# Start-up fills, weight loads, masked copies and the last products of a fused recurrence, gated MLP and attention kernel

## The chip, the cores and the metric

The kernel runs on one core of a Trainium2 chip. The metric is the device time of one launch in microseconds (us). The engines are called as in the profile: PE is TensorE, DVE is VectorE, ACT is ScalarE, POOL is GpSimd, and SP is SyncE, which issues nearly all transfers.

## The reference

Three stages follow each other. B = 4 batches, H = 8 heads, S = 768 positions, D = 48 channels a head.

```
state = 0                                    # per batch and head, 48 x 48
for t in range(S):                           # 1: a gated linear recurrence
    cur = outer(u * k[t], v[t])
    y[t] = r[t] @ (state + cur)
    state = w[t][:, None] * state + outer(k[t], v[t])
x = y of all heads, as (B, S, 384)
h = relu(x @ w_in)                           # 2: 384 -> 1024
c = 3-tap convolution of h along S, one filter a channel
x = (h * sigmoid(c)) @ w_out                 # 1024 -> 384
logits = x @ w_gate                          # 3: attention with 4 experts, the best 2 of 4 a row
out = sum over e of w[e] * (softmax(causal(q[e] k[e]^T / 8)) @ v[e]) @ wo[e]
```

## The kernel before

**Stage 1 and 2 (`phase1`).** The recurrence is computed in chunks of 128 positions. A unit is one batch, one half of the sequence (3 chunks) and one pair of heads: 32 units, `u` = 0 to 31, each in a slot of code (`slot`, line 559). All engines follow the written order there (`manual_schedule`): an engine takes its instructions strictly one after another. For a unit, `load` (line 129) brings one tile `wkr` of 1156 columns: 388 of decays w, 384 of k, 384 of r. DVE scans the decays forward (`scan_d`, tile Dp, with the constants cD) and backward (`scan_f`, tile Fp, with cF), and multiplies them into Q and K. In each slot PE transposes K (`trans`, line 327, into a tile `m`), multiplies k*r by u (`m<-u_c,wkr`, the bonus of the own position, only for u < 12), forms the 6 score blocks (`scores`, into two one-bank tiles `sc`), the state (`state`) and the output of the unit before (`yout`). ACT puts the bonus on the diagonal of a tile AT (`blocks`, 6 instructions for u < 6). DVE then lays the scores above it where a mask allows (`masked`, line 322): two copies with a predicate, 128x384 each, one a head. At the end of each slot ACT and DVE cut the output of the unit before into a high and a low part (`rows`), and SP moves it into X.

The weights arrive raw (`load_w`, 768 KB pieces, tile `rawt`) and are converted in the slots around: `conv0_w` and `conv1_w` on DVE, ACT and POOL, `conv2_w` on ACT, `conv3_w` on DVE. From slot 5 on the MLP's products run between these (`mlp1`, line 436; `mlp2`, line 513). `slot` prepares unit u+1 while it finishes unit u.

**Before the first slot** POOL fills cD, cF, a tile of ones for the mask and the four state tiles Ss (lines 172 to 186). SP issues the loads of units 0, 1 and 2 (each `wkr` in two pieces), the small `u_c` (0.8 KB in runs of 4 bytes), `u_b`, and, from slot 0, the first raw weights.

**Stage 3 (`Attention.run`).** Sixteen units `j`, each two heads and one half of the rows. The order is a scheduler's, not written out. `soft` forms scores in a tile `st` (two banks, two buffers), DVE adds the mask and takes the minimum, ACT exponentiates into A. For the unit before, `transp` multiplies A by the row's factor `rs`, transposes it on PE (tile `t`) and copies it out as T; `av` multiplies by V; `proj_out` (line 1142) multiplies the high and low parts of the result O by two parts of `wo`, six products a row block, and stores a block of the output. The multiplication of A by `rs` is on DVE up to unit 12 and on POOL from unit 13 (`SCALED_ON_POOL`, line 46).

```
1112            if self.unit >= SCALED_ON_POOL:
1113                nc.gpsimd.tensor_tensor(at, at, rs[:, q:q + 1].to_broadcast(...), op=OP.mult)
1115                nc.vector.tensor_scalar(at, at, rs[:, q:q + 1], None, op0=OP.mult)
```

Of the kernel before, what the change touches and what calls it, by code (L numbers as in the profile page):

```python
# [23 lines left out]
C = 128  # L24
# [19 lines left out]
EARLY = 8  # L44
CARRY_ON_PE = 8
SCALED_ON_POOL = 13
# [60 lines left out]
def phase1(tc, nc, a, x2, ident, stat, lim, top, right, left2, at):  # L107
# [5 lines left out]
    ps_s = s1.enter_context(tc.tile_pool(name="ps_s", bufs=2, space=PSUM, side="left"))  # L113
# [15 lines left out]
    def load(u):  # L129
        b, h, hp = split(u)  # L130
        q = b * HP + hp
        x = ld.tile([128, NWKR], F32, name="wkr")
        if u not in (0, 1, 2, 28, 29, 30, 31):
# [33 lines left out]


    cD = cst.tile([128, CH, C + 1], F32, name="cD")
    cF = cst.tile([128, CH, C + 1], F32, name="cF")  # L170
    with tc.manual_schedule(engines={mybir.EngineType.Pool}):
        nc.gpsimd.memset(cD, 0.0)
        nc.gpsimd.memset(cD[:, :, 0:1], 1.0)
        nc.gpsimd.memset(cD[:, :, C:C + 1], TINY)  # L174
        nc.gpsimd.memset(cF, 0.0)
    ones3 = wk.tile([128, CH, C], F32, name="Q")
    nc.gpsimd.memset(ones3, 1.0)
    nc.gpsimd.affine_select(ones3, ones3, pattern=[[0, CH], [1, C]], compare_op=OP.is_gt, fill=0.0, base=0,
                            channel_multiplier=-1)
    msk = cst.tile([128, CH, C], U32, name="msk")  # L180
    nc.vector.tensor_copy(msk, ones3)
    Ss = []
    for i in range(HP):
        t = cst.tile([128, NC - 1, 64], F32, name=f"Ss{i}")
        nc.gpsimd.memset(t, 0.0)
        Ss.append(t)
# [3 lines left out]
    for u in (1, 2):  # L190
        load(u)
        load_v(u)
    u_b = cst.tile([128, HP, 2, D], F32, name="u_b")
    nc.sync.dma_start(u_b, bass.AP(tensor=a["u"].tensor, offset=a["u"].offset, ap=[[0, 128], [1, H * D]]))

# [29 lines left out]
    RW = {}  # L225

# [86 lines left out]
    def scores(u):  # L313
        t = T[u]
        sc = [ps_s.tile([128, CH, C], F32, name="sc") for j in range(2)]
        for c in range(CH):
            for j in range(2):
                p = slice(64 * j, 64 * j + 64)
                nc.tensor.matmul(sc[j][:, c], t["K"][p, c], t["Q"][p, c], start=True, stop=True)  # L319
        t["sc"] = sc  # L320

    def masked(u):
        t = T[u]
        for j, sc in enumerate(t["sc"]):
            nc.vector.copy_predicated(t["AT"][:, j], msk, sc)

    def trans(u):
        b, h, hp = split(u)
        t = T[u]
        n = CH - h  # L330
        m = ps_m.tile([128, CH * 128 + 2 * CH], F32, name="m")
        kt = m[:, 0:CH * 128].rearrange("p (c t) -> p c t", c=CH)
        for c in range(n):
            nc.tensor.transpose(kt[:, c], t["K"][:, c], ident)
        KT = t["KT"] = wk.tile([128, CH, 128], F32, name="KT")
        if u < BONUS_ON_PE:
            es = m[:, CH * 128:].rearrange("p (j c) -> p j c", j=2)
            for c in range(CH):
                nc.tensor.matmul(es[:, :, c], t["r"][:, c], u_c[:, hp], start=True, stop=True)
# [219 lines left out]
    def slot(u):  # L559
# [3 lines left out]
        for z, n, m in WS + WC2:  # L563
            if u == z - 1:
                load_w(n, m)
# [90 lines left out]
        if EARLY <= u < 2 * NU:  # L656
            check(u, 1)
# [12 lines left out]
    with tc.manual_schedule(engines=mine):  # L670
        scan_d(0)
# [236 lines left out]
class Attention:  # L908
    def __init__(self, tc, nc, a, x2, out, ident):
# [33 lines left out]

    P3 = ((0, 0), (0, 1), (1, 0))
# [163 lines left out]
    def transp(self, A, rs, T, qi):  # L1108
# [32 lines left out]

    def proj_out(self, b, O, t):
        nc = self.nc
        pt = self.ps_m.tile([128, 512], F32, name="m")
        m = 0
        for p in range(2):
            for oi, wi in self.P3:
                nc.tensor.matmul(pt[:, 0:DM], O[oi][:, p, t * C:(t + 1) * C], self.wo[wi][:, p], start=(m == 0),  # L1148
                                 stop=(m == 5))
                m += 1  # L1150
        ot = self.ap.tile([128, DM], F32, name="ot", bufs=3)
        if t in OUT_ON_DVE:
            nc.vector.tensor_copy(ot, pt[:, 0:DM])
        else:
            nc.scalar.activation(ot, pt[:, 0:DM], AF.Copy)
        nc.sync.dma_start(self.out[b, t * C:(t + 1) * C], ot)

    def run(self):
# [41 lines left out]
        def tail(j):  # L1200
# [4 lines left out]
            for e in range(2):  # L1205
                for q in range(3):
                    def f(e=e, q=q):
# [4 lines left out]
                        self.unit = j  # L1212
# [157 lines left out]
```

## Time and profile before

| | |
|---|---|
| median of 3 runs | 599.38 us (599.34 to 600.6) |
| profiled execution, its own time | 599.62 us |
| span of its instructions | 597.9 us |
| PE busy, its instructions | 567.4 us (95%), 4386 |
| PE weight loads busy | 508.6 us (85%) |
| DVE busy | 495.7 us (83%) |
| ACT busy | 397.1 us (66%) |
| POOL busy | 172.8 us (29%) |
| q1, the data queue | 89.53 MB, 51.7% of 16 engines |

The times of the profile are those of one execution, counted from the start of its span; its own time is 1.72 us more than its span. An engine's share over the whole span mixes stages with different limits, so shares are read by stretch. A row of the timeline gives start, duration, engine, line of the code, operation, tiles written and read, and a count.

### The profile page before, as it was taken

How to read it: one execution, taken by the hardware profiler on the slowest of the kernel's cores; microseconds unless marked ns; L12 is line 12 of the kernel's file. 1: busy time of each engine (PE TensorE's matmuls, PEld its weight loads, DVE VectorE, ACT ScalarE, POOL GpSimd, SP SyncE). 2: the span in 40 equal slices, each digit the busy share in tenths (PEclk: the TensorE clock that was granted, in tenths of full speed). 3: DMA queues.
4: the chain of work that ended last, by engine and by line, in shares of the span. 5: the costliest groups of instructions: out<-in, count | busy, mean ns of one | idle time of the engine just before them, and what ended most of it. 6: DMA issues, size and time to landing. Idle time of an engine off the chain costs nothing.

```text
span 597.9 us, 12391 instructions
## 1 busy us (share of the span) xinstructions
PE 567.4 (95%) x4386; PEld 508.6 (85%) x4386; DVE 495.7 (83%) x1153; ACT 397.1 (66%) x1015; POOL 172.8 (29%) x246
## 2 busy tenths in 40 slices
PE   4898989999999999999999999999999999999986
PEld 4686888999999999989999999697889787988644
DVE  6999999999999999999966865988767865875751
ACT  4986656767777788887776764766656565655622
POOL 3565552335435342424400000400120021004250
PEclk9759889999999999999999999999999999999999
DMA  7676425664747868676453436760476053605202
GB/s 237 229 253 208 161 77 143 191 172 125 223 123 225 295 198 285 205 225 185 128 139 101 118 87 166 201 143 1 121 198 158 28 130 96 145 28 147 67 1 86
DMA packets 47158, 90.41 MB, mean 151 GB/s; under 512 B 14320, under 2 KB 28656, under 8 KB 47088
## 3 DMA queue, kind: packets, MB, share of 16 engines
q1 hardware_dynamic: 47088, 89.53, 51.7%
q8 instruction: 37, 0.61, 0.4%
q14 instruction: 33, 0.27, 0.2%
HBM read 50.23 MB, written 9.44 MB: 100 GB/s over the span
## 4 chain that ended last, share of the span: by engine, by line
PE 65%; DVE 15%; ACT 7%; DMA 6%; issue 3%; POOL 2%; SPq 2%; ACTq 0%; DVEq 0%; POOLq 0%
PE hs L447 11%; PE x L521 11%; PE m L1012 8%; PE st L1086 6%; PE t L1120 5%; PE m L1136 5%; PE m L1042 4%; PE m L1148 3%; PE sc L319 2%; DMA sl<-kl 2%; DVE Dp L258 2%; PE m L397 2%; PE m L405 2%; DVE Fp L266 1%; PE m L352 1%
## 5 line engine op out<-in xcount | busy, mean ns | idle before, releaser
L447 PE MATMUL hs<-X,win 128*128 128x384 f32 (+1 forms) x576 | 118.4, 350 | 1.0 <-ACT ht L451 1.0
L447 PEld LDWEIGHTS hs<-X,win 128*128 128x128 f32 x576 | 99.2, 189 | 3.8 <-ACT ht L451 1.7
L521 PE MATMUL x<-gh,wout 128*128 128x386 f32 (+1 forms) x384 | 100.1, 342 | 0.0
L1100 ACT ACTIVATE A<-sm,mn 128x128 f32<-128x128 f32 (+5 forms) x96 | 63.7, 664 | 27.6 <-DVE mn L1099 27.6
L484 ACT ACTIVATE st<-ct 128x382 f32<-128x382 f32 (+1 forms) x64 | 33.7, 526 | 69.5 <-DVE ct L479 35.8
L1099 DVE CUSTOM_DVE_ANT_0 sm<-st,mask 128x128 f32<-128x128 f32 (+5 forms) x96 | 58.1, 619 | 22.6 <-PE st L1086 19.3
L302 POOL TENSOR_SCALAR_AFFINE_SELECT AT<-e 128x384 f32<-128x384 f32 x52 | 43.6, 859 | 108.9 <-DVE e L292 107.8
L521 PEld LDWEIGHTS x<-gh,wout 128*128 128x128 f32 x384 | 71.7, 193 | 0.0
L521 PE MATMUL x<-gl,wout 128*128 128x382 f32 (+1 forms) x192 | 65.6, 342 | 0.0
L1120 PE MATMUL t<-ident,A 128*128 128x128 f32 x336 | 53.2, 275 | 2.8 <-ACT T L1124 1.6
L1120 PEld LDWEIGHTS t<-ident,A 128*128 128x128 f32 x336 | 39.8, 140 | 10.0 <-issue 4.1
L1126 DVE COPY T<-t 128x128 f32<-128x128 f32 (+3 forms) x64 | 32.2, 503 | 18.4 <-PE t L1120 18.0
L1136 PE MATMUL m<-T,V 128*64 128x384 f32 (+2 forms) x288 | 45.9, 422 | 0.4 <-ACT T L1124 0.2
L1086 PE MATMUL st<-sk,sq 128*128 128x384 f32 (+3 forms) x128 | 43.8, 353 | 0.8 <-DVE mn L1099 0.5
L1086 PE MATMUL st<-sl,sq 128*128 128x384 f32 (+3 forms) x128 | 40.7, 328 | 2.8 <-DMA sl<-kl 2.7
L493 DVE SCALAR_TENSOR_TENSOR st<-st,ht 128x382 f32<-128x382 f32 (+1 forms) x64 | 36.4, 569 | 7.1 <-ACT st L484 5.4
L1124 ACT ACTIVATE T<-t 128x512 f32<-128x512 f32 (+3 forms) x64 | 28.5, 445 | 20.7 <-PE t L1120 20.4
L258 DVE TENSOR_TENSOR_SCAN Dp<-wkr,cD 128x387 f32<-128x387 f32 x32 | 39.1, 1221 | 3.6 <-POOL cD L174 3.6
L455 ACT ACTIVATE ct<-ht,cwk 128x382 f32<-128x382 f32 (+1 forms) x64 | 39.5, 618 | 2.1
L310 ACT ACTIVATE Fp<-wkr,lim 128x384 f32<-128x384 f32 x64 | 38.8, 607 | 0.3
L1136 PEld LDWEIGHTS m<-T,V 128*64 128x64 f32 x288 | 21.6, 136 | 20.2 <-issue 14.1
L508 DVE TENSOR_TENSOR gl<-st,gh 128x382 fp32r<-128x382 f32 (+1 forms) x64 | 35.6, 557 | 1.8 <-ACT gh L500 1.6
(148 smaller groups left out, 1316.4 us busy)
## 6 DMA issues: line engine op xcount, KB each, us to landing
wkr<-in_wkr SPq DMA_DIRECT2D x25, 578.0 KB, 4.2
v<-in_rkv SPq DMA_DIRECT2D x32, 192.0 KB, 4.1
rawt<-in_win SPq DMA_DIRECT2D x8, 768.0 KB, 6.1
rawt<-in_wout SPq DMA_DIRECT2D x8, 768.0 KB, 5.8
sk<-kh SPq DMA_DIRECT2D x32, 192.0 KB, 3.4
sl<-kl SPq DMA_DIRECT2D x32, 192.0 KB, 4.0
rn<-in_rkv SPq DMA_DIRECT2D x20, 288.0 KB, 3.7
x<-x SPq DMA_DIRECT2D x12, 384.0 KB, 4.3
```

Of the source, the lines that this page charges most:

```text
L258: nc.vector.tensor_tensor_scan(fl(t["Dp"]), t["w"][:, 0:NW], fl(cD), 0.0, op0=OP.mult, op1=OP.add)
L302: nc.gpsimd.affine_select(AT[:, j], t["e"][:, j][:, :, None].to_broadcast([128, CH, C]), pattern=[[0, CH], [1, C]], compare_op=OP.is_equal ...
L310: nc.scalar.activation(Fp[:, :, 0:C], wc, AF.Relu, bias=lim[:, z:z + 1], scale=(-1.0, 1.0)[z], accum_out=stat[:, 2 * u + z:2 * u + z + 1])
L447: nc.tensor.matmul(hs[:, 0:N], win[wi][:, f // 2, i, (f % 2) * 128:(f % 2 + 1) * 128], x[:, i, xi], start=(n == 0), stop=(n == 8))
L455: nc.scalar.activation(ct, ht[:, o:o + N], AF.Copy, scale=w[:, 1, f:f + 1])
L521: nc.tensor.matmul(acc[0][i][:, 0:N], wout[wi][:, f, i * 128:(i + 1) * 128], G[g][gi], start=(f == 0 and z == 0), stop=(f == NF - 1 and z ...
L1012: nc.tensor.matmul(pt[:, 0:HT], w[wi][:, i, p * 128:(p + 1) * 128], xs[xi][:, i, s], start=(m == 0), stop=(m == 8))
L1086: nc.tensor.matmul(st[:, z, 0:n], q[:, qi * C:(qi + 1) * C], k[:, z * n:(z + 1) * n], start=(i == 0), stop=(i == 1))
L1099: nc.vector.tensor_tensor_reduce(o3, i3, m3, 1.0, 3e38, op0=OP.add, op1=OP.min, accum_out=mn)
L1100: nc.scalar.activation(at, o3, AF.Exp, bias=mn, scale=-1.0, accum_out=rs[:, qi % 3:qi % 3 + 1])
L1120: nc.tensor.transpose(pt[:, ki - k0], at[:, ki * C:(ki + 1) * C], self.ident)
L1136: nc.tensor.matmul(po[o, lo:HT], V[:, ki, (2 * p + j) * 64:(2 * p + j + 1) * 64], Ts[j][:, ki, lo:], start=(ki == 0), stop=(ki == n - 1))
```

## The change

1. **Constants and mask.** DVE instead of POOL fills the ones, cD and cF. POOL keeps the triangular select that makes the mask of the ones, and the four Ss. The cast of the mask (`msk`) moves ahead of the first scan on DVE.
2. **Loads.** `wkr` of units 1 and 2 goes in one transfer each, and that of unit 1 stands ahead of v and u_c. The first raw weights stand right behind `wkr` of unit 2, before slot 0, and their first conversion moves within slot 1, to behind `keys`. `u_b` is loaded in slot 2. `wkr` of units 24 to 27 goes in two pieces instead of one.
3. **Unit 0 on PE.** The products with u_c come ahead of the transposes.
4. **Masked copy.** Both heads' scores lie in one tile of two banks, and one copy of 128x768 takes the place of two of 128x384 in all 32 units.
5. **Scaling of A.** POOL keeps only the first head of units 14 and 15, (14, 0) and (15, 0); unit 13 and the second heads of 14 and 15 go to DVE.
6. **Last products.** Of the last row group, nine of the eighteen products (those of the first pair of heads) are formed when the tail of the last unit begins, in the two `st` tiles. The other nine follow the last `av`, high parts first. The three blocks are evacuated by ACT, DVE and ACT; the third is stored from ACT's queue.

```
-EARLY = 8
-SCALED_ON_POOL = 13
+SCALED_ON_POOL = ((14, 0), (15, 0))
...
+    with tc.manual_schedule(engines={mybir.EngineType.Pool, mybir.EngineType.DVE}):
+        nc.vector.memset(ones3, 1.0)
+        nc.vector.memset(cD, 0.0)
+        nc.vector.memset(cD[:, :, 0:1], 1.0)
+        nc.vector.memset(cD[:, :, C:C + 1], TINY)
+        nc.vector.memset(cF, 0.0)
     load(0)
+    load(1)
     load_v(0)
...
+    load(2)
+    load_w("win", 0)
+    load_v(1)
+    load_v(2)
...
-        sc = [ps_s.tile([128, CH, C], F32, name="sc") for j in range(2)]
+        sb = ps_s.tile([128, 2, 512], F32, name="sc")[:, :, 0:CH * C]
+        sc = [sb[:, j].rearrange("p (c t) -> p c t", c=CH) for j in range(2)]
...
-        for j, sc in enumerate(t["sc"]):
-            nc.vector.copy_predicated(t["AT"][:, j], msk, sc)
+        nc.vector.copy_predicated(t["AT"].rearrange("p j c t -> p j (c t)"),
+                                  fl(msk)[:, None, :].to_broadcast([128, 2, CH * C]), t["sc"])
...
-            if u == z:
+            if u == z and u > 1:
                 conv0_w(n, m)
...
+        if u == 1:
+            conv0_w("win", 0)
...
-        if self.unit >= SCALED_ON_POOL:
+        if self.unit in SCALED_ON_POOL:
...
+    def proj_sum(self, pt, O, t, p, parts=P3):
+        for oi, wi in parts:
+            self.nc.tensor.matmul(pt, O[oi][:, p, t * C:(t + 1) * C], self.wo[wi][:, p],
+                                  start=(p == 0 and (oi, wi) == (0, 0)), stop=(p == 1 and oi == 1))
...
+            if j == NJ - 1:
+                pts = []
+                def early():
+                    z = [self.ps_s.tile([128, 2, 512], F32, name="st") for _ in range(2)]
+                    for t in range(3):
+                        pts.append(z[t % 2][:, t // 2, 0:DM])
+                        self.proj_sum(pts[t], OS[b], 3 * h + t, 0)
+                def final():
+                    for parts in self.P3[0:2], self.P3[2:3]:
+                        for t in range(3):
+                            self.proj_sum(pts[t], OS[b], 3 * h + t, 1, parts)
+                    ots = [self.ot(pts[t], t == 1) for t in (0, 1, 2)]
+                    for t in range(3):
+                        queue = self.nc.scalar if t == 2 else self.nc.sync
+                        queue.dma_start(self.out[b, (3 * h + t) * C:(3 * h + t + 1) * C], ots[t])
+                todo.insert(0, early)
+                todo.append(final)
```

The start of DVE's order before, up to the first products of unit 1 (Q on the mask's row is the tile of ones, which shares its name with the queries):

```order
L258 SCALAR_TENSOR_TENSOR Dp<-wkr,cD 128x387
L261 RECIPROCAL cF<-Dp 128x3
L278 TENSOR_TENSOR Q<-wkr,Dp 128x384
L181 CAST msk<-Q 128x384
L266 SCALAR_TENSOR_TENSOR Fp<-wkr,cF 128x387
```

And the same start of DVE's order now:

```order
L162 MEMSET Q 128x384
L163 MEMSET cD 128x387
L164 MEMSET cD 128x3
L165 MEMSET cD 128x3
L166 MEMSET cF 128x387
L676 CAST msk<-Q 128x384
L249 SCALAR_TENSOR_TENSOR Dp<-wkr,cD 128x387
L252 RECIPROCAL cF<-Dp 128x3
```

Five fills and the cast of the mask now stand ahead of the first scan.

SP's first transfers now (before, lines 137 to 205 in this order: `wkr` of unit 0 in two, v, u_c, `wkr` of units 1 and 2 in two pieces with a v behind each, u_b, raw weights):

```order
L136 DMA wkr<-in_wkr 128x388
L136 DMA wkr<-in_wkr 128x768
L133 DMA wkr<-in_wkr 128x1156
L144 DMA v<-in_rkv 128x384
L173 DMA u_c<-in_u 48x4x1 x2
L133 DMA wkr<-in_wkr 128x1156
L192 DMA rawt<-in_win 128x768
L144 DMA v<-in_rkv 128x384 x2
```

The whole `wkr` of unit 1 has moved to before u_c, and the raw weights to before the v of unit 1.

PE's order now, from the last scores of the last unit (`st<-sl`) to the next transposes (A_7480 and A_7550 are the two heads of unit 14); before, eleven transposes stood here in a row:

```order
L1094 MATMUL st<-sl_7304,sq_7218 128x384
L1152 MATMUL st<-wo_4383,O_7469 128x384
L1152 MATMUL st<-wo_4384,O_7469 128x384
L1152 MATMUL st<-wo_4383,O_7470 128x384
...
L1128 MATMUL t<-ident,A_7480 128x128 x5
L1152 MATMUL st<-wo_4383,O_7469 128x384
L1152 MATMUL st<-wo_4384,O_7469 128x384
L1152 MATMUL st<-wo_4383,O_7470 128x384
L1128 MATMUL t<-ident,A_7480 128x128 x2
L1128 MATMUL t<-ident,A_7550 128x128 x4
```

Nine products with `wo` (three more stand at the "...") now lie among the transposes of unit 14.

DVE's order there now, with the copies T<-t of the transposes and the multiplications of A (`TENSOR_SCALAR A`), which were on POOL:

```order
L1114 TENSOR_TENSOR rs<-rs,ex 128x3
L1123 TENSOR_SCALAR A_7550<-A_7550,rs 128x512
L1123 TENSOR_SCALAR A_7550<-A_7550,rs 128x640
L1123 TENSOR_SCALAR A_7550<-A_7550,rs 128x768
L1112 TENSOR_SCALAR rs<-rs 128x3
L1113 RECIPROCAL rs<-rs 128x3
L1114 TENSOR_TENSOR rs<-rs,ex 128x3
L1107 ISA sm,mn<-st,mask 128x256
L1107 ISA mn 128x1
L1134 COPY T_7625<-t 128x4x128
L1148 TENSOR_TENSOR O_7470<-m,O_7469 128x384
L1107 ISA sm,mn<-st,mask 128x384
```

The last two maskings (`sm<-st`), which free the two `st` tiles, stand behind three multiplications that were not on this engine.

## Rows read from the trace of the kernel before

**Rows 1.** Busy time by stretch: stretch, PE, PEld, DVE, ACT, POOL, PEclk, DMA, GB/s
```profile
20.00:110.00 90.00, 80.61 (x663) 71.95 (x661) 88.73 (x151) 63.02 (x169) 47.51 (x64) 0.83 0.54 171
110.00:222.00 112.00, 111.94 (x1051) 106.15 (x1050) 110.67 (x207) 81.95 (x208) 49.13 (x60) 1.00 0.66 197
```

**Rows 2.** Chain of waits, 60 to 222 us: start, duration, engine, tile, line
```profile
118.33 1.48 DVE Dp L258
...
133.06 1.78 PE hs L447 x9
```

**Rows 3.** Chain of waits, 7 to 20 us
```profile
6.90 0.48 DVE K L273
...
7.51 0.87 PE m L334 x3
...
12.69 1.09 PE m L339 x6
...
14.24 1.85 ACT AT L300 x6
...
20.00 1.51 DVE Dp L258
```

**Rows 4.** Timeline of the first 8 us; in brackets the idle time before and its end
```profile
0.81 0.87 SPq L137 DMA_DIRECT2D wkr<-in_wkr  x2
...
1.50 0.42 POOL L172 MEMSET cD<- 128x387 f32 x1
...
2.20 0.92 SPq L164 DMA_DIRECT2D u_c<-in_u  x2
...
3.62 0.96 DVE L258 TENSOR_TENSOR_SCAN Dp<-wkr,cD 128x387 f32<-128x387 f32 x1 [3.62 <-POOL cD L174]
3.88 1.01 POOL L178 TENSOR_SCALAR_AFFINE_SELECT Q<-Q 128x384 f32<-128x384 f32 x1
...
5.23 0.35 DVE L181 CAST msk<-Q 128x384 uint32<-128x384 f32 x1
```

**Rows 5.** DMA issues, 0 to 3.15 us: size of each, us from issue to landing
```profile
wkr<-in_wkr SPq DMA_DIRECT2D x1, 384.0 KB, 3.2
wkr<-in_wkr SPq DMA_DIRECT2D x1, 194.0 KB, 2.4
...
u_c<-in_u SPq DMA_DIRECT2D x2, 0.8 KB, 2.9
```

**Rows 6.** Timeline of DVE, 72 to 74 us
```profile
72.01 0.95 DVE L95 SCALAR_TENSOR_TENSOR wm<-rawt,wm 128x768 int32<-128x768 int32 x1
72.88 1.07 DVE L325 COPY_PREDICATED AT<-msk,sc 128x384 f32<-128x384 uint32 x2
73.83 0.55 DVE L418 TENSOR_TENSOR Y<-m,Y 128x384 fp32r<-128x384 f32 x1
```

**Rows 7.** Busy time by stretch, line 325 (masked copies) alone
```profile
20.00:110.00 90.00, 9.49 (x18) 0.83 0.54 171
```

**Rows 8.** Busy time by stretch, 570 to 580 us
```profile
570.00:580.00 10.00, 7.58 (x48) 4.86 (x48) 5.95 (x13) 3.42 (x8) 5.71 (x8) 1.00 0.00 1
```

**Rows 9.** Waits, 568 to 580 us: who for whom, us in total, times, longest
```profile
PEld t L1120 <- POOL A L1113: 2.4, 3, 1.0
```

**Rows 10.** Timeline, 561.7 to 571 us
```profile
567.05 1.37 DVE L1106 TENSOR_TENSOR rs<-rs,ex 128x3 f32<-128x3 f32 x1
...
568.57 3.68 POOL L1113 TENSOR_TENSOR A<-A,rs 128x512 f32<-128x512 f32 x3 [0.16 <-DVE rs L1106]
```

**Rows 11.** Groups of DVE by form, 330 to 598 us: count, busy us, mean ns
```profile
L1115 DVE TENSOR_SCALAR A<-A,rs 128x768 f32<-128x768 f32 x12 | 7.4, 615 | 0.0
```

**Rows 12.** Timeline of the end
```profile
588.55 3.78 PE L1148 MATMUL m<-wo,O 128*128 128x384 f32 x18
...
592.37 0.49 ACT L1155 ACTIVATE ot<-m 128x384 f32<-128x384 f32 x1 [0.50 <-PE m L1148]
```

**Rows 13.** DMA issues after 592.4 us
```profile
out_dram<-ot SPq DMA_DIRECT2D x1, 192.0 KB, 3.0
```

More of the change, by code (lines that the diff above doesn't have):

```diff
@@ L112, in phase1 @@
     wk = s1.enter_context(tc.tile_pool(name="wk", bufs=3, side="left"))
-    ps_s = s1.enter_context(tc.tile_pool(name="ps_s", bufs=2, space=PSUM, side="left"))
+    ps_s = s1.enter_context(tc.tile_pool(name="ps_s", bufs=1, space=PSUM, side="left"))
     ps_m = s1.enter_context(tc.tile_pool(name="ps_m", bufs=2, space=PSUM, side="left"))
@@ L132, in load @@
         x = ld.tile([128, NWKR], F32, name="wkr")
-        if u not in (0, 1, 2, 28, 29, 30, 31):
+        if 0 < u < 24:
             nc.sync.dma_start(x, a["wkr"][q, h])
@@ L156, in load_rk @@
                                   for o in (0, 2 * CH * D))
+    cD = cst.tile([128, CH, C + 1], F32, name="cD")
+    cF = cst.tile([128, CH, C + 1], F32, name="cF")
+    msk = cst.tile([128, CH, C], U32, name="msk")
+    ones3 = wk.tile([128, CH, C], F32, name="Q")
+    with tc.manual_schedule(engines={mybir.EngineType.Pool, mybir.EngineType.DVE}):
[4 more added lines that the diff above has]
+        nc.vector.memset(cF, 0.0)
     load(0)
+    load(1)
     load_v(0)
@@ L166, in phase1 @@
     wide = a["win"].dtype == U64
[L169 to L181, printed above, removed]
     Ss = []
     for i in range(HP):
-        t = cst.tile([128, NC - 1, 64], F32, name=f"Ss{i}")
-        nc.gpsimd.memset(t, 0.0)
-        Ss.append(t)
+        Ss.append(cst.tile([128, NC - 1, 64], F32, name=f"Ss{i}"))
     Bd = []
@@ L189, in phase1 @@
         Bd.append(cst.tile([128, NC - 1, 128], F32, name=f"Bd{i}"))
-    for u in (1, 2):
-        load(u)
-        load_v(u)
     u_b = cst.tile([128, HP, 2, D], F32, name="u_b")
-    nc.sync.dma_start(u_b, bass.AP(tensor=a["u"].tensor, offset=a["u"].offset, ap=[[0, 128], [1, H * D]]))
     WC = 2 * DM
@@ L332, in trans, with sums @@
         kt = m[:, 0:CH * 128].rearrange("p (c t) -> p c t", c=CH)
+        es = m[:, CH * 128:].rearrange("p (j c) -> p j c", j=2)
+        def sums():
+            for c in range(CH if u < BONUS_ON_PE else 0):
+                nc.tensor.matmul(es[:, :, c], t["r"][:, c], u_c[:, hp], start=True, stop=True)
+        if u == 0:
+            sums()
         for c in range(n):
             nc.tensor.transpose(kt[:, c], t["K"][:, c], ident)
+        if u:
+            sums()
         KT = t["KT"] = wk.tile([128, CH, 128], F32, name="KT")
         if u < BONUS_ON_PE:
-            es = m[:, CH * 128:].rearrange("p (j c) -> p j c", j=2)
-            for c in range(CH):
-                nc.tensor.matmul(es[:, :, c], t["r"][:, c], u_c[:, hp], start=True, stop=True)
             e = t["e"] = wk.tile([128, 2, CH], F32, name="e")
@@ L563, in slot @@
         for z, n, m in WS + WC2:
-            if u == z - 1:
+            if u == z - 1 and u:
                 load_w(n, m)
@@ L589, in slot @@
             check(u, 0)
-            if u >= EARLY:
+            if u >= CARRY_ON_PE:
                 scores(u)
@@ L610, in slot @@
             bonus(u + 2)
-        if u < EARLY:
+        if u < CARRY_ON_PE:
             scores(u)
             state(u)
-            for c in range(CH - u // HP % 2 if u < CARRY_ON_PE else 1):
+            for c in range(CH - u // HP % 2):
                 scaled(u, c)
@@ L649, in slot @@
             load_cw()
+        if u == 2:
+            nc.sync.dma_start(u_b, bass.AP(tensor=a["u"].tensor, offset=a["u"].offset, ap=[[0, 128], [1, H * D]]))
         for z, n, m in WC2:
@@ L655, in slot @@
         groups(ga + 1)
-        if EARLY <= u < 2 * NU:
+        if CARRY_ON_PE <= u < 2 * NU:
             check(u, 1)
@@ L670, in phase1 @@
     with tc.manual_schedule(engines=mine):
+        nc.gpsimd.affine_select(ones3, ones3, pattern=[[0, CH], [1, C]], compare_op=OP.is_gt, fill=0.0, base=0,
+                                channel_multiplier=-1)
+        nc.vector.tensor_copy(msk, ones3)
+        for t in Ss:
+            nc.gpsimd.memset(t, 0.0)
         scan_d(0)
@@ L908 @@
 class Attention:
+    P3 = ((0, 0), (0, 1), (1, 0))
     def __init__(self, tc, nc, a, x2, out, ident):
@@ L942, in open_right @@
         self.ps_s = R("ps2_s", 2, space=PSUM)
-    P3 = ((0, 0), (0, 1), (1, 0))
     def stage(self, pool, n):
@@ L1140, in av, with ot @@
         nc.vector.tensor_tensor(O[1][:, p, s], po[:, 0:HT], _f(O[0][:, p, s]), op=OP.subtract)
+    def proj_sum(self, pt, O, t, p, parts=P3):
+        for oi, wi in parts:
+            self.nc.tensor.matmul(pt, O[oi][:, p, t * C:(t + 1) * C], self.wo[wi][:, p],
+                                  start=(p == 0 and (oi, wi) == (0, 0)), stop=(p == 1 and oi == 1))
     def proj_out(self, b, O, t):
         nc = self.nc
-        pt = self.ps_m.tile([128, 512], F32, name="m")
-        m = 0
+        pt = self.ps_m.tile([128, 512], F32, name="m")[:, 0:DM]
         for p in range(2):
[L1147 to L1150, printed above, removed]
+            self.proj_sum(pt, O, t, p)
+        self.nc.sync.dma_start(self.out[b, t * C:(t + 1) * C], self.ot(pt, t in OUT_ON_DVE))
+    def ot(self, pt, on_dve):
+        nc = self.nc
         ot = self.ap.tile([128, DM], F32, name="ot", bufs=3)
-        if t in OUT_ON_DVE:
-            nc.vector.tensor_copy(ot, pt[:, 0:DM])
-        else:
-            nc.scalar.activation(ot, pt[:, 0:DM], AF.Copy)
-        nc.sync.dma_start(self.out[b, t * C:(t + 1) * C], ot)
+        if on_dve:
+            nc.vector.tensor_copy(ot, pt)
+        else:
+            nc.scalar.activation(ot, pt, AF.Copy)
+        return ot
     def run(self):
@@ L1211, in f @@
                             Ts.append(ap.tile([128, 3 * (h + 1), HT], F32, name=f"T{h}", bufs=2))
-                        self.unit = j
+                        self.unit = j, e
                         self.transp(A, rs, Ts[e], 3 * h + q)
@@ L1221, in tail @@
             half[b, h] = half.get((b, h), 0) + 1
-            if half[b, h] == 2:
+            if j == NJ - 1:
[15 more added lines that the diff above has]
+                todo.append(final)
+            elif half[b, h] == 2:
                 for t in range(3):
```

2 lines of the change are left out of this document (1 added, 1 removed).

## The prediction, made before the run

> **What bounds the kernel now.** I read the stretches first, then the chain of waits, then the timeline at the two ends. The chain is DVE's up to about 120 us and PE's behind that: at 118.33 it still runs through a scan of DVE, and from there to 222 us its long pieces are products such as the one at 133.06 [rows 2]. The stretches agree. From 20 to 110 us DVE is busy 88.73 of 90 us and PE 80.61; from 110 to 222 us PE is busy 111.94 of 112 us, with DVE close behind at 110.67 [rows 1]. So a microsecond taken from DVE before 110 us is worth about a microsecond, and one taken from it later almost nothing. Ahead of that, in the first 20 us, the chain goes DVE (K of unit 0), PE (7.51 to 13.78), ACT (the six diagonal blocks at 14.24 and what follows them), and comes back to DVE with the scan at 20.00 [rows 3]. The last place is the tail: from 570 to 580 us PE is busy only 7.58 of 10 us [rows 8], and its transposes wait 2.4 us in total for A scaled by POOL [rows 9].
>
> **First unit.** The first scan starts at 3.62, released by a fill of POOL [rows 4]; its data, the 194 KB piece issued at 0.81, landed 2.4 us later, at 3.21 [rows 4, 5]. DVE's new fills have no row. From above, three large ones at POOL's 0.42 and two small ones that I count with them as a fourth are 1.7 us; from below, at the cast's 0.35, they are 1.2 [rows 4]. DVE stands idle until 3.62 and the engines begin near 0.8, so they end between 2.0 and 2.5. POOL reaches its select at 1.50, where its first large fill stood; the select takes 1.01 and the cast 0.35, together until 2.9 [rows 4]. Both sides end ahead of 3.21, so the fills cost nothing and the data is late next: 0.41 saved. The cast leaves the path behind the scan: 0.3. K of unit 0, ready at 7.38 [rows 3], comes near 6.7.
>
> PE can't take all of it, since its first instructions are now the products with u_c. The second piece of u_c was issued at 2.66 (half of 0.92 behind 2.20) and landed about 2.9 later, near 5.6 [rows 4, 5]. Now the 578 KB of unit 1's tile stand ahead of it. Their price: the 384 KB piece, issued 0.44 behind the 194 KB one, landed at 4.45 against 3.21, which is 1.24 us for 384 KB; 578 KB at that rate are 1.9 us, and u_c lands at 7.5. That is one end, a gain of nothing against the old start at 7.51; the other end is K itself, 6.85, a gain of 0.65. Unbroken rows and a busier stream should do better than that one interval, so I take 7.2 and a **gain of 0.3**. From there on PE, ACT and DVE run as in [rows 3], each shifted by this: the order within the chain is the same, as products and transposes only changed places. The wait for raw weights in slot 1 goes too, but DVE would then only stand longer in front of the high part that ACT makes at the end of that chain, so I count nothing for it. u_b, read only from unit 12 on, and the extra splits of units 24 to 27 cost an issue on SP, which the loads' lead of two to three slots hides; without that lead it would be half a microsecond each.
>
> **Masked copy.** The pair of 128x384 copies holds DVE from 72.88 to 73.83, 0.95; the 128x768 instruction of two inputs before it from 72.01 to 72.88, 0.87 [rows 6]. So one copy for two saves 0.08. No row shows a predicated copy across two banks or with a repeated mask: from the other side it could cost what the pair costs (saving 0), and from below it could save the whole second start, 0.15. I take 0.09, nearest to [rows 6]. Between 20 and 110 us there are 18 copies, nine units [rows 7], where DVE sets the pace: 9 x 0.09 = **0.8**. The 23 other units lie where PE, or in the first two the chain of [rows 3], does; nothing is counted. The scores of the next unit now wait for the whole copy instead of its first half; PE has 9 us of slack in that stretch [rows 1] to hide 0.4 a unit.
>
> **Tail, the scaling.** On POOL three multiplications took 3.68; DVE needs at most 3 x 0.615 = 1.85 for the same three [rows 10, 11]. The second head of unit 14, ready at 572.25 before (568.57 + 3.68), would be ready near 570. Unit 13's move changes little, since the scores that follow wait for transfers. PE then loses most of its 2.4 us of waiting [rows 9], but nine products come into the same place: 18 took 3.78 [rows 12], so nine are 1.9. They also wait for the last masking on DVE, which now stands behind the three multiplications; I give that 0.5. What remains is a gain of 2.4 + 0.9 (other idle time in [rows 8], once the copies follow sooner) - 1.9 - 0.5, near **1.0**, with ends at 0 and 2.4.
>
> A row bears on the multiplications that stay on POOL: an addition-sized product of DVE, 3 elements a row, took 1.37 us at 567.05 and ended as POOL's first head ended [rows 10]. The Trainium skill, GPSIMD Engine Reference, section Key points, says that POOL shares its SBUF interfaces with VectorE and that the two contend when DVE has two SBUF inputs or a two-port mode. The trace agrees; by the rule the multiplications now on DVE wait for POOL in the same way, which is my slower rival below, and where they don't overlap the sum stays.
>
> **Tail, the end.** Behind the last av PE had 18 products, 588.55 to 592.33; the last evacuation runs 592.37 to 592.86 and the last store lands 3.0 us after its issue [rows 12, 13]. Now nine remain (1.9), but the first must wait for the high part by ACT, a step like the 0.49 of [rows 12] plus a hand-over, 0.6; before, products of the first pair filled that time. Two evacuations on ACT in a row are 1.0, where one was visible. So 3.78 + 0.5 becomes 0.6 + 1.9 + 1.0: 0.8 saved, and another 0.2 as evacuations overlap with products. Three stores now start within a microsecond; by [rows 13] the last is alone, so I add 0.4 to its landing. **Gain 0.6**, ends 0 and 1.3. On the store from ACT's queue: the row shows 3.0 us of landing, of which the issue is a part; the Trainium skill, DMA: Bandwidth & Descriptors, section Issuing engines are not separate DMA queues, says that a second issuing engine saves only issue time. By the rule nothing of the landing goes, and without it the sum would be about 1 us better.
>
> **Sum.** 0.3 + 0.8 + 1.0 + 0.6 = 2.7. From the profiled execution's 599.62 (597.9 and 1.7 around it) that gives 596.9. The median of the runs is 0.24 lower than that execution, so I predict 596.7. Added ends: 0 + 0 + 0 + 0 at one side, 0.65 + 1.35 + 2.4 + 1.3 = 5.7 at the other.
>
> **Rivals.** (a) *The tail hides nothing*: the nine products and the scaling on DVE eat each other's gain up to av, and only 0.3 + 0.8 remain with little at the end: 598.3. For it: the transposes also wait for their copies, not only for POOL. Against: 2.4 us of waiting on POOL alone. (b) *DVE paces the middle too*: all 31 later copies count, 2.5 instead of 0.8, time 595.0. For it: DVE is busy 110.67 of 112 us; against: the chain there is PE's alone. (c) *u_c comes late*: its runs of 4 bytes move slowly behind full tiles, PE starts near 8.2, the first term is -0.7 and the time 597.7. Here the first part doesn't do what it says: DVE is early and PE is not. (d) *Slower: DVE becomes the bound of the tail.* Place: its queue from 567 us on, with the copies that PE's transposes need behind six multiplications. Price: 1.85 and, for the small three, 0.9, and one lock-out of 1.2 (1.37 less the usual 0.16), and the 1.9 of products no longer hidden: 5.9 against 2.4 taken away, so +3.5, less 0.3 + 0.8 + 0.6: 601.2. It decides when DVE falls behind by over 4 us there; DVE is busy 5.95 of 10 us in that stretch [rows 8], which speaks against it.
>
> **Chances.** Forecast 0.60, (a) 0.14, (b) 0.11, (c) 0.09, (d) 0.06. About 0.2% (1.2 us) is what a measurement of this kernel can tell from no change, so faster is under 598.2: the forecast, (b) and (c), 0.80; same is (a), 0.14; slower (d), 0.06. The likeliest's own range is 595.6 to 597.9. With parts of (a) and (b) the range is 594.8 to 598.6.
>
> **What would show it.** In the changed profile: the first scan at 3.2 to 3.3, released by its data; PE's first product between 6.9 and 7.5 and released by u_c; the scan of unit 3 near 19.7; one copy of about 0.95 duration and 0.87 to the next instruction; the first MLP-bound chain piece about 1.1 us earlier; PE above 8.5 of 10 us in the stretch that was 570 to 580; the last av's end 1.5 to 2.5 us earlier, and 3.3 us from there to the last store's issue. I am wrong if PE starts later than 7.6, if the chain at 130 us is not earlier by a microsecond, or if the transposes of unit 14 wait for DVE as long as they waited for POOL.

## The result and the profile after

The changed kernel is slower: 603.41 us (median of 11 runs, 600.51 to 605.47) against 600.60 for the kernel before beside it, ratio 1.0052, 95% interval 1.0036 to 1.0068. A second series gave 1.0040 (1.0025 to 1.0056). The forecast was 596.7, a ratio of 0.9955. The profiled execution took 603.16 with a span of 601.4, 3.4 more than before.

Where the time went is read from marks in both traces: PE's first product, the starts of DVE's first scan of each unit, and later the ends of the MLP's last `x` product, of the last av and of the span.

| mark | before | after | difference |
|---|---|---|---|
| PE's first product | 7.51 | 8.90 | +1.39 |
| scan of unit 3 | 20.00 | 21.36 | +1.36 |
| scan of unit 6 | 42.69 | 45.58 | +2.89 |
| scan of unit 12 | 108.96 | 111.95 | +2.99 |
| scan of unit 31 | 290.16 | 294.00 | +3.84 |
| MLP's last product, end | 357.78 | 361.30 | +3.52 |
| last av, end | 588.62 | 591.93 | +3.31 |
| end of the span | 597.91 | 601.35 | +3.44 |

The stretches of [rows 1] and [rows 8], as they stand after (the last one shifted by the 3.5 us; columns as there):
```profile
20.00:110.00 90.00, 75.44 (x646) 66.90 (x647) 86.94 (x138) 61.85 (x167) 47.89 (x62) 0.85 0.55 172
...
573.50:583.50 10.00, 9.07 (x60) 6.62 (x60) 5.77 (x17) 4.03 (x10) 1.75 (x3) 1.00 0.01 2
```
DVE, which paces the first stretch, is busy 86.94 us there instead of 88.73: it stands still more. In the tail PE is busy 9.07 of 10 us instead of 7.58, above the 8.5 that was forecast. But 2.0 of it are the nine early products, and only 0.2 us of the 3.5 comes back by the last av.

**The head.** Timeline, and under it the DMA issues (size, us from issue to landing), of the changed kernel, against [rows 3 to 5]:
```profile
2.22 1.25 DVE L676 CAST msk<-Q 128x384 uint32<-128x384 f32 x1
3.41 0.96 DVE L249 TENSOR_TENSOR_SCAN Dp<-wkr,cD 128x387 f32<-128x387 f32 x1
...
6.53 0.55 DVE L264 TENSOR_TENSOR K<-wkr,Fp 128x384 f32<-128x384 f32 x1
...
8.90 1.41 PE L329 MATMUL m<-u_c,wkr 128*128 128x2 f32 x6 [8.90 <-DVE Dp L249]
...
13.41 1.05 DVE L316 COPY_PREDICATED AT<-msk,sc 128x768 f32<-128x768 uint32 x1 [2.14 <-ACT AT L291]
...
21.36 1.51 DVE L249 TENSOR_TENSOR_SCAN Dp<-wkr,cD 128x387 f32<-128x387 f32 x1
```
```profile
wkr<-in_wkr SPq DMA_DIRECT2D x1, 578.0 KB, 6.1
v<-in_rkv SPq DMA_DIRECT2D x1, 192.0 KB, 6.2
u_c<-in_u SPq DMA_DIRECT2D x1, 0.8 KB, 5.9
```
DVE is early, but a little less than forecast: the scan at 3.41 follows the cast, which ends at 3.47 where 2.9 was reckoned, and not its data, which had landed at 3.3. K is done at 7.08 instead of 7.38. PE is not early. The product needs r*k of unit 0, done at 6.6, and the two pieces of u_c. The scan named as its releaser, unit 1's, ends at 8.82 by chance: in run 2 PE starts while that scan has not begun. What ended last is u_c, issued at 2.67 and 3.15 and landed at 8.6 and 8.8, 5.6 to 5.9 us behind the issue instead of 2.9.

**The slots of units 4 and 5.** DVE's two waits, then the issues behind which they stand:
```profile
37.17 0.96 DVE L249 TENSOR_TENSOR_SCAN Dp<-wkr,cD 128x387 f32<-128x387 f32 x1 [0.59 <-POOL wm L95]
39.65 0.56 DVE L83 TENSOR_SCALAR wm<-rawt 128x768 int32<-128x768 int32 x1 [1.52 <-DMA rawt<-in_wout]
```
```profile
u_b<-in_u SPq DMA_DIRECT2D x1, 192.0 KB, 4.5
wkr<-in_wkr SPq DMA_DIRECT2D x1, 578.0 KB, 5.8
rawt<-in_wout SPq DMA_DIRECT2D x1, 768.0 KB, 7.8
```
u_b now goes out in slot 2 (issue at 30.68), ahead of unit 5's tile (31.30) and the raw weights (31.80). The raw weights land at 39.6 and DVE, ready at 38.1, stands 1.5 us. The difference to the kernel before goes from 1.4 us at unit 3 to 2.9 at unit 6.

**The masked copy.** DVE around one copy, as in [rows 6]:
```profile
43.32 0.95 DVE L94 SCALAR_TENSOR_TENSOR wm<-rawt,wm 128x768 int32<-128x768 int32 x1
44.19 1.03 DVE L316 COPY_PREDICATED AT<-msk,sc 128x768 f32<-128x768 uint32 x1
45.12 0.54 DVE L417 TENSOR_TENSOR Y<-m,Y 128x384 fp32r<-128x384 f32 x1
```
0.93 to the next instruction, where the pair took 0.95 and the forecast wanted 0.87. Between the scans of units 6 and 11 the difference stays within 0.04 us: nothing is gained there.

**The tail.** Scaling, early products, and the long av; then the end, with the last stores:
```profile
566.39 3.68 POOL L1121 TENSOR_TENSOR A<-A,rs 128x512 f32<-128x512 f32 x3 [67.29 <-DVE rs L1114]
...
571.38 1.48 DVE L1123 TENSOR_SCALAR A<-A,rs 128x512 f32<-128x512 f32 x3
...
575.56 1.23 PE L1152 MATMUL st<-wo,O 128*128 128x384 f32 x6
...
577.09 0.77 PE L1152 MATMUL st<-wo,O 128*128 128x384 f32 x3
...
582.78 3.44 PE L1144 MATMUL m<-T,V 128*64 128x384 f32 x22
...
592.52 1.83 PE L1152 MATMUL st<-wo,O 128*128 128x384 f32 x9 [0.59 <-ACT O L1147]
594.22 0.56 DVE L1166 COPY ot<-st 128x384 f32<-128x384 f32 x1 [1.16 <-PE st L1152]
594.44 0.87 ACT L1168 ACTIVATE ot<-st 128x384 f32<-128x384 f32 x2 [1.97 <-PE st L1152]
594.96 1.43 SPq L1251 DMA_DIRECT2D out_dram<-ot  x2
595.34 0.40 ACTq L1251 DMA_DIRECT2D out_dram<-ot  x1
```
The second head of unit 14 is scaled by DVE in 1.48 us, by 572.86, and PE's wait for POOL is gone. Behind the last av the evacuations end after 3.38 us (591.93 to 595.31) instead of 4.24; the forecast was 3.3. The store on ACT's queue lands at 598.1, 2.8 behind its issue. SP's second store, issued at 595.40, is the last to land, 3.2 later at 598.6, and the span ends 2.8 us behind that. Before, it ended 2.0 behind the last landing (592.9 + 3.0) [rows 12, 13]. In the eight profiles with the old end the last store lands 7.3 us behind the last av in the mean and the span ends 1.9 to 2.5 us later (mean 2.2); in the eight with the new end it lands after 6.9 us and the span ends 2.2 to 4.5 us later (mean 2.9). So the output lands 0.4 us sooner, and more than that is lost behind the last landing. What the program does there, no row names.

### The profile page after: what moved, and what is told of

Its sections match the earlier page's. It is cut to its first block, busy times and chain, and to the rows that moved or that the text cites. A ratio compares the mean times of both kernels' runs of the same rounds, so it can differ in the third digit from the quotient of the medians.

```text
span 601.4 us, 12351 instructions
## 1 busy us (share of the span) xinstructions
PE 562.5 (94%) x4386; PEld 504.8 (84%) x4386; DVE 500.0 (83%) x1139; ACT 397.7 (66%) x1014; POOL 160.7 (27%) x229
## 4 chain that ended last, share of the span: by engine, by line
PE 57%; DVE 21%; ACT 9%; DMA 7%; issue 3%; SPq 2%; ACTq 0%; DVEq 0%
PE hs L446 10%; PE x L520 9%; PE m L1020 8%; PE st L1094 6%; PE m L1144 6%; PE t L1128 5%; PE m L1050 4%; DMA sl<-kl 3%; PE m L1152 3%; DVE Dp L249 3%; DVE Fp L257 2%; DVE ct L465 2%; PE sc L311 2%; DMA v<-in_rkv 2%; DVE ct L478 2%
## 5 line engine op out<-in xcount | busy, mean ns | idle before, releaser
L446 PE MATMUL hs<-X,win 128*128 128x384 f32 (+1 forms) x576 | 120.2, 354 | 0.3 <-ACT ht L450 0.2
L446 PEld LDWEIGHTS hs<-X,win 128*128 128x128 f32 x576 | 101.0, 192 | 3.2 <-ACT ht L450 1.0
L1128 PEld LDWEIGHTS t<-ident,A 128*128 128x128 f32 x336 | 40.1, 140 | 8.4 <-issue 3.8
L249 DVE TENSOR_TENSOR_SCAN Dp<-wkr,cD 128x387 f32<-128x387 f32 x32 | 37.7, 1178 | 1.4 <-DMA wkr<-in_wkr 0.8
```

Source lines behind the costliest of these rows:

```text
L249: nc.vector.tensor_tensor_scan(fl(t["Dp"]), t["w"][:, 0:NW], fl(cD), 0.0, op0=OP.mult, op1=OP.add)
L446: nc.tensor.matmul(hs[:, 0:N], win[wi][:, f // 2, i, (f % 2) * 128:(f % 2 + 1) * 128], x[:, i, xi], start=(n == 0), stop=(n == 8))
L1128: nc.tensor.transpose(pt[:, ki - k0], at[:, ki * C:(ki + 1) * C], self.ident)
```

## Experiments

Ratios are to the kernel before, run beside each on the same chip. A profile shows one execution; a ratio comes from several.

**1. The same kernel again.**

> The changed kernel itself once more, to see which of its differences come back. Theory A (the order of the transfers costs the time): PE starts at 8.9 and the scan of unit 3 near 21.4 again, DVE waits 1.5 us for raw weights near 38 again, ratio to the kernel before 1.004 to 1.007. Theory B (the low-clock stretches of PE between 20 and 115 us fall differently by chance and make the difference): the stretches lie elsewhere this time and the time moves by over 2 us from the recorded 603.2 of the profiled run, with the same start. The 0.6 us that were lost between 389 and 536 us are not in either theory; if they are absent here they were chance.

1.0040 (1.0025 to 1.0056). PE starts at 9.14, the scan of unit 3 at 21.62, DVE waits 1.38 us for raw weights at 40.1: what the loads do comes back. Chance adds to it: DVE also waits 1.58 us for ACT near 55, which the first profile did not show (run 9 tells why). The loss in the attention stage that the expectation names is there again: from the MLP's end to the copy of the ninth av's result it takes 0.55 us more than before, in the first profile 0.71. What makes it stays open.

**2. u_c early.**
```diff
     load(0)
+    u_c = ...; two loads of u_c
     load(1)
     load_v(0)
-    u_c = ...; two loads of u_c
```


> The changed kernel with the two small loads of u_c issued directly behind unit 0's tile, ahead of unit 1's 578 KB. Theory A: u_c lands near 5, PE's first product starts at 6.6 (it then waits for r*k) instead of 8.9, the scan of unit 3 starts at 19.3 to 19.8 instead of 21.4, and the whole is 1.2 to 2.0 us faster than the changed kernel, about 601.5. Theory B: the start comes earlier by as much, but DVE's later wait for raw weights or PE's low clock takes it back, and the time is within 0.6 us of the changed kernel's.

1.0021 (1.0005 to 1.0038), 1.1 us better than run 1. Timeline:
```profile
6.63 1.41 PE L329 MATMUL m<-u_c,wkr 128*128 128x2 f32 x6 [6.63 <-DVE wkr L280]
8.00 0.96 DVE L249 TENSOR_TENSOR_SCAN Dp<-wkr,cD 128x387 f32<-128x387 f32 x1 [1.00 <-DMA wkr<-in_wkr]
...
19.75 1.52 DVE L249 TENSOR_TENSOR_SCAN Dp<-wkr,cD 128x387 f32<-128x387 f32 x1
```
PE starts when DVE's r*k is there, and the scan of unit 3 comes 1.6 us sooner. Theory A holds for the start; of its lead only 0.6 us is left at unit 6, since DVE then waits 1.39 us ahead of unit 5's scan and 1.60 for raw weights that take 8.8 us behind u_b.

**3. u_b late.**
```diff
-        if u == 2:
+        if u == 7:
             nc.sync.dma_start(u_b, ...)
```


> The changed kernel with the 192 KB load of u_b in slot 7 instead of slot 2. Theory A: the raw weights that are issued near 32 us land within 6.5 us instead of 7.8, DVE's wait of 1.5 us near 38 goes, the scan of unit 6 starts near 44.2 instead of 45.6, and the time falls by 1.0 to 1.5 us, to about 602. Theory B: the wait only moves to the next slot's raw weights (the kernel before had 0.4 us there) and the time falls by less than 0.5 us.

1.0014 (0.9999 to 1.0029), 1.6 us better than run 1. DVE no longer waits for raw weights, and unit 6's scan starts at 44.26. Their landing, and one wait that came in the place of the old one, at the first `hs` products:
```profile
rawt<-in_wout SPq DMA_DIRECT2D x1, 768.0 KB, 5.5
```
```profile
53.96 0.71 DVE L465 SCALAR_TENSOR_TENSOR ct<-ht,cwk,ct 128x381 f32<-128x381 f32 x1 [1.59 <-ACT ct L454]
```

**4. Both loads moved.** Both edits together.

> The changed kernel with both loads moved: u_c directly behind unit 0's tile, u_b in slot 7. Theory A (the two loads are the loss, and the rest of the change is worth nothing net before the tail): PE starts at 6.6, the scan of unit 3 at 19.7, unit 6 near 42.3 (before: 42.69), no wait of over 0.5 us for raw weights before 60 us, and a ratio to the kernel before of 0.997 to 1.000. Theory B (each repair alone gave 1.2 to 1.5 us, but they overlap): ratio 1.001 or more. By the sum of the prediction with the masked copy at nothing and the end at nothing, 0.3 + 1.0 would be left: 0.998.

0.9974 (0.9957 to 0.9990): 0.66% or 4.0 us better than run 1. By the intervals this is 2.6 to 5.4 us, so it agrees with the sum of the two (2.7). The loss is the order of these two loads; without it the change is a gain. The marks of theory A were missed in part: PE starts at 6.81 and no wait for raw weights over 0.5 us is left, but unit 3's scan starts at 20.77 and unit 6's at 43.42. Unit 1's tile, one transfer of 578 KB, lands 6.3 us behind its issue and DVE waits for it:
```profile
9.01 0.96 DVE L249 TENSOR_TENSOR_SCAN Dp<-wkr,cD 128x387 f32<-128x387 f32 x1 [1.83 <-DMA wkr<-in_wkr]
```
Run 8, with the same loads, had 0.89 us of this wait, and the scans at 19.48 and 42.12.

**5. The old end.** The block for the last unit is taken out, so that all output tiles go through `proj_out` as before.

> The changed kernel with the last products as in the kernel before (18 behind the last av, three stores one after the other as each row block is ready); all else as changed. If the new end costs 0.2 us net, as one profile of each showed (span end 9.5 us behind the last av's end against 9.3), the time stays within 0.5 us and the span ends 9.2 to 9.4 us behind the last av's end; what the nine early products cost PE ahead of the last long av shows as that av coming up to 0.5 us earlier. If the new end is worth the 0.6 us of the prediction, the time rises by 0.6.

1.0038 (1.0022 to 1.0054): no difference that this measurement can tell. In the profile the last av ends 0.9 us sooner behind the MLP (229.73 us against 230.63), and the span ends 9.9 us behind it instead of 9.4. The interval of this comparison is about 1.3 us to either side, so it excludes neither the prediction's 0.6 nor a loss of 1.

**6. The scalings alone**, on the kernel before.
```diff
-SCALED_ON_POOL = 13
+SCALED_ON_POOL = ((14, 0), (15, 0))
-        if self.unit >= SCALED_ON_POOL:
+        if self.unit in SCALED_ON_POOL:
...
-                        self.unit = j
+                        self.unit = j, e
```


> The kernel before with one edit: of the scalings by POOL only the first heads of units 14 and 15 stay there, the other heads are scaled by DVE. The prediction's sum gives 2.4 + 0.9 of PE's idle time in the tail without the nine early products, so 2.0 to 3.0 us off, ratio 0.995 to 0.997. The slower rival (DVE becomes the bound of the tail) gives no gain or a loss. From the profiles of the changed kernel (0.9 us off up to the last av with 1.9 us of early products put in) and of the one with the old end (1.2 off), 0.9 to 1.2 us: ratio 0.998.

0.9967 (0.9954 to 0.9980), 2.0 us off. From the MLP's last product to the last av's end it takes 229.19 us instead of 230.84. A repeat (run 11) gave 0.9967 again.

**7. One masked copy alone**, on the kernel before (one `sc` tile of two banks, one copy).

> The kernel before with one edit: both heads' scores in one tile of two banks and one masked copy a unit. By the prediction 0.09 us for each of nine units between 20 and 110 us: 0.8 us off, ratio 0.9987. By the changed kernel's rows (one copy to the next instruction 0.93 to 0.95, the pair before 0.94 to 0.95) nothing is saved, and the scores of the next unit wait for the whole copy: ratio 1.000 to 1.001, with the scans of units 7 to 12 as far apart as before.

1.0002 (0.9988 to 1.0015). The next instruction follows 0.93 us behind the copy here, 0.90 to 0.93 before 120 us:
```profile
73.11 1.03 DVE L325 COPY_PREDICATED AT<-msk,sc 128x768 f32<-128x768 uint32 x1
74.04 0.54 DVE L419 TENSOR_TENSOR Y<-m,Y 128x384 fp32r<-128x384 f32 x1
```
That is 0.02 to 0.05 a unit, 0.2 to 0.45 in nine. The scans of units 3 and 12 are 88.76 us apart instead of 88.96; as the five profiles with two copies have 88.60 to 89.07, that mark can't tell it from nothing, and neither can the time.

**8. Another mask**, one execution.
```diff
-        m2 = fl(msk)[:, None, :].to_broadcast([128, 2, CH * C])
+        m2 = A2.bitcast(U32) if u % 2 else fl(msk)[:, None, :].to_broadcast([128, 2, CH * C])
```


> The changed kernel with both loads moved; in odd units the masked copy reads a full mask of 768 numbers a row (the destination's own bits) in place of the mask of 384 that is read twice, so that the masking of odd units isn't the reference's. If the repeated mask costs the second start, odd units take 0.87 from the copy's start to the next instruction's, as two-input instructions of that width in SBUF do, and even units 0.93 to 0.95. If the two banks of PSUM cost it, or this operation is so by itself, both take the same.

Odd and even units take the same, 0.92 to 0.96. The repeated mask is not what costs the second start; whether the two banks are, was not tried.

**9. The parts together**: the changed kernel with both loads moved, unit 1's tile in two pieces and the old end.

> The changed kernel with what the runs so far speak for: u_c behind unit 0's tile, unit 1's tile in two pieces as in the kernel before, u_b in slot 7, the scalings as changed, and the old end. Theory A (the parts add): the head 0.2 to 0.5 us ahead of the kernel before at the scan of unit 3, 0.3 from the one copy by 110 us, 2.0 from the scalings: 2.5 to 2.8 us off, ratio 0.9953 to 0.996. Theory B (what the head and the copy give is lost again before PE becomes the bound): the scalings alone, ratio 0.9967.

0.9970 (0.9957 to 0.9982), no better than the scalings alone. The scan of unit 3 starts at 19.34, 0.66 us early, unit 6's at 42.00; then the lead is lost. PE and DVE, and for comparison the same products in the kernel before:
```profile
47.22 3.25 PE L446 MATMUL hs<-X,win 128*128 128x384 f32 x9
...
51.67 0.70 DVE L465 SCALAR_TENSOR_TENSOR ct<-ht,cwk,ct 128x381 f32<-128x381 f32 x1 [1.58 <-ACT ct L454]
```
```profile
41.00:51.50 10.50, 9.51 (x61) 8.13 (x61) 9.09 (x13) 6.06 (x16) 7.97 (x11) 0.51 0.63 218
```
```profile
47.80 1.84 PE L447 MATMUL hs<-X,win 128*128 128x384 f32 x9
```
Nine products take 3.25 us instead of 1.84, as the granted clock is 1.2 GHz there (mean 0.51 from 41 to 51.5 us, the third number from the end of the row), and DVE waits for what ACT makes of them. PE had been busy 1.19 us of 38 to 40 and 0.38 of 40 to 42, where the clock fell. In the kernel before the same products ran at 2.4 GHz (1.84 us; granted clock 1.00 from 48 to 50). This too differs from execution to execution: of the two profiles with this head in run 11, one has a wait of 1.39 us there and unit 7's scan at 51.95, the other no wait and 50.99.

**10. Only the first unit**: fills on DVE, the cast behind the select, products with u_c first; all transfers as in the kernel before.

> The kernel before with the fills on DVE, the cast behind POOL's select and, in unit 0, the products with u_c ahead of the transposes; all transfers in the order of the kernel before. The prediction's term without the late u_c: the first scan at 3.4, PE's first product at 6.5 to 6.8 instead of 7.51, the scan of unit 3 at 19.4 to 19.8 instead of 20.00, and 0.2 to 0.6 us off the whole, ratio 0.999 to 0.9997. If raw weights or unit 2's tile come late in the head, the scan of unit 3 stays at 20.0 and the ratio at 1.000.

0.9988 (0.9977 to 0.9999): 0.7 us off, though the scan of unit 3 is late, at 21.28:
```profile
6.51 1.41 PE L332 MATMUL m<-u_c,wkr 128*128 128x2 f32 x6 [6.51 <-DVE wkr L284]
...
14.22 0.56 DVE L84 TENSOR_SCALAR wm<-rawt 128x768 int32<-128x768 int32 x1 [1.75 <-DMA rawt<-in_win]
...
18.18 1.78 DVE L67 SCALAR_TENSOR_TENSOR cm<-cr,cm 128x24 f32<-128x24 uint32 x1
```
```profile
18.12 1.80 POOL L96 TENSOR_TENSOR wm<-wm,wy 128x768 int32<-128x768 int32 x1 [4.17 <-DVE cex L62]
```
PE's start is 1.0 us early. DVE then waits 0.7 longer for the raw weights, and a DVE instruction on 24 columns, 0.18 us in the kernel before, takes 1.78, from just behind the start of a POOL instruction to its end. Neither expectation foresaw that. In the other fifteen profiles this instruction takes 0.18. Unit 4's scan starts at 28.58, 0.65 late, and the span in this profile is 0.6 longer than before: one profile does not show where the 0.7 us of the runs come from, and their interval only just leaves out no change.

**11. The new end, twice.** First on the kernel before with the scalings:

> The kernel before with the scalings of the changed kernel and its end (nine products early in the score banks, nine at the end, three stores together). From the profiles so far the early products cost about 1.0 us of PE ahead of the last av, and the end behind it is 0.1 us shorter: the gain of 0.9967 for the scalings alone falls to 0.998 to 0.9985. If the end were worth what the prediction gave it (0.6 behind the last av, with the nine products hidden), the ratio would be 0.9957.

1.0015 (1.0001 to 1.0029), where the scalings alone had 0.9967: 2.9 us, across two series. In its profile the last av comes 1.0 us later behind the MLP (230.19 us against 229.19) and the span ends 11.5 us behind it instead of 9.3 to 9.6, 4.5 of them behind the last landing. As this and run 5 disagreed, the repaired kernel of run 9 was run again with and without the end, beside the scalings alone:

> The repaired kernel once more (u_c early, unit 1's tile in two pieces, u_b in slot 7, scalings as changed, old end), beside the two it is compared with. If the head (0.66 us at the scan of unit 3) and the copy (0.03 to 0.04 us a unit) reach the end, it is 0.6 to 1.0 us faster than the kernel before with the scalings alone; if the stretches of low clock that follow decide when PE's own chain begins, the two are within 0.5 us.

0.9973 (0.9961 to 0.9985).

> The same with the end of the changed kernel put back. If the end's net is the early products' 1.0 us less 0.1 behind the last av, as the profiles so far show: 0.6 to 1.2 us slower than the repaired kernel. If the prediction's term holds (0.6 gained behind the last av, the early products hidden): 0.6 us faster.

0.9998 (0.9987 to 1.0008): the end costs 0.25%, 1.5 us. The three comparisons of the end give 0.1, 2.9 and 1.5 us of loss, and none the forecast gain.

> The kernel before with the scalings alone, once more: ratio to the kernel before 0.9955 to 0.998 again, the last av 1.8 us earlier behind the end of the MLP than in the kernel before.

0.9967 (0.9953 to 0.9982). The repaired head is again no faster than this. Both traces of the scalings alone are equal up to unit 12's scan (108.97 and 109.07), but unit 13's starts at 118.25 in the first and at 119.10 in the second, and 1 us remains to the end of the MLP. The stretches of the first, and of the second:
```profile
80.00:86.00 6.00, 5.68 (x29) 5.60 (x29) 6.00 (x12) 4.37 (x12) 0.81 (x1) 0.72 0.08 30
93.00:99.00 6.00, 5.90 (x39) 5.82 (x40) 6.00 (x13) 3.90 (x12) 1.05 (x3) 1.00 0.38 144
```
```profile
80.00:86.00 6.00, 5.65 (x37) 5.27 (x38) 6.00 (x12) 4.71 (x14) 0.85 (x1) 1.00 0.09 30
93.00:99.00 6.00, 5.91 (x31) 5.83 (x31) 6.00 (x13) 3.44 (x10) 0.19 (x1) 0.72 0.52 179
```
The last stretch at the low clock falls at 82 us in one execution and at 94 in the other, and the second is 1 us longer. All sixteen profiles go this way: in the eleven whose last low stretch lies between 80 and 90 us, unit 13's scan starts 9.27 to 9.39 us behind unit 12's, and in the five where it lies between 92 and 100 us, 10.03 to 10.07. Those five include the first profile of the changed kernel, so 0.8 of the 0.85 that the table shows between units 12 and 31 is of this kind and not of the change. I read it so: with a stretch that late, PE has no time left to catch up before it becomes the bound near 110 us; no run sets the clock, so this is not shown. Nor do these rows show what places the stretch. Ahead of the falls PE was busy 0.61 of 2 us from 78 to 80 in the first and 1.21 and 1.20 of 2 us from 90 to 94 in the second, but in the first it was busy only 1.04 of 2 us from 92 to 94 and the clock stayed.

## Why the prediction was wrong

**First unit, "I take 7.2 and a gain of 0.3": the step that failed most.** The first scan's start was nearly right (the fills were not free: the cast took 1.25 us instead of 0.35, so the scan began at 3.41 instead of 3.2 to 3.3), and so was the release of PE by u_c. The price for unit 1's tile was not: one interval of 1.24 us between two landings was read as the time of 384 KB in a queue. In the changed kernel that tile, unit 0's v and u_c were issued between 1.72 and 3.15 and all landed between 7.8 and 8.8. With the tile ahead of it u_c landed at 8.76 instead of 5.47: 3.3 us for 578 KB, where 1.9 was reckoned. That the transfers take from one another is how I read it; no run separates them. So the bound of 7.5 was no bound, rival (c) had the right outcome (8.2), and the size was 8.9, later than the 7.6 that was named as a sign of being wrong. The term came out at -1.4 (+0.3 forecast); moving u_c took 1.1 us off (run 2).

**"Cost an issue on SP, which the loads' lead of two to three slots hides": failed.** I priced the issue of u_b and not its 192 KB. The raw weights behind it took 7.8 us instead of 5.5 (run 3), and DVE was ready 1.4 us before they landed. 1.6 us (run 3), forecast at nothing. With u_c that is 4.0 us by run 4, more than the whole loss.

**Masked copy, 0.8: mis-sized.** At most 0.2 to 0.45 us by the rows of run 7, and nothing that the time shows. The single instruction of two inputs in SBUF [rows 6] was the wrong neighbour: this copy keeps nearly all of the cost of the pair, the end of the range where the term is nothing.

**Scaling, net 1.0: near, by luck, from two wrong sizes.** From the MLP's last product to the last av's end, the mean is 231.12 us over three profiles with the scalings of before (230.8 to 231.6), 229.37 over five with them changed and the old end (229.2 to 229.7), and 230.38 over eight with the new end (230.2 to 230.6). So the scalings give 1.75, where 3.3 was reckoned, and the nine early products cost 1.0 of it, where 2.4 was: net 0.7. Rival (d) did not happen; DVE was busy 5.77 of 10 us there.

**The end, 0.6: failed.** The evacuations end 0.86 sooner behind the last av (1.0 was worked out), and the last store lands 0.4 sooner in the mean. But the span does not follow: it ended 9.2 to 9.9 us behind the last av in eight profiles with the old end and 9.2 to 11.5 in eight with the new one. The step took for granted that the span ends as long behind the last landing as before, and it ended 0.7 later in the mean; the cause of that stays open. With the 1.0 of early products the end is a loss, 1.5 us in the comparison side by side (run 11). The products moved forward were counted under the tail and the gain behind av under the end, and neither was asked whether they pay each other.

**The sum.** -1.4 for the first unit, -1.6 for u_b, about +0.2 for the copy, +0.7 for the scaling with the early products and -0.5 for the rest of the end give -2.6; the two series of the changed kernel measured -2.4 and -3.1. In the prediction, the lower price of the fills should be 1.4 by its own count, not 1.2, and rival (b) takes 0.08 a copy where the forecast takes 0.09; nothing hangs on either.

**The slower case** had 0.06. Its named mechanism was not the one that came: a transfer put ahead of others, twice, which I had as a rival of 0.7 us and as a cost of nothing.

## What to carry to other kernels

A load that is put ahead of others is charged with its bytes, not with its issue: list what is in flight then, and who waits for the last of it. Work moved off the end onto an earlier place of the same engine is paid there unless a row shows that engine idle for as long. Where a head start meets a stretch in which the clock differs from execution to execution, look for the next mark behind it before counting the gain.

## What was not expected of the hardware

- Behind unit 0's tile, a piece of 0.8 KB landed 5.9 us behind its issue with a further 578 KB and 192 KB ahead of it, 3.1 to 3.4 us behind without them (run 2).
- The cast to the mask took 1.25 us on DVE while POOL filled other tiles (2.22 to 3.47, the fills 1.98 to 3.26), 0.35 before; the instruction on 24 columns of run 10 took 1.78 instead of 0.18 beside one of POOL, and ended with it.
- The same program, with the same times to within 0.1 us at 109 us, ended its MLP 1 us apart, the later one with its last stretch of low clock at 94 us instead of 82.
